# An expert layer with one first-stage product: relu(x(w1-w2)) w_out + x(w2 w_out) in place of max(x w1, x w2) w_out

## The chip, the core and the metric

One core of a Trainium2 chip runs the whole kernel. The metric is the device time of one execution in microseconds (us). TensorE (PE) multiplies, VectorE (DVE) and ScalarE (ACT) move results out of PSUM and do elementwise work, GpSimd (POOL) and SyncE (SP) here mostly issue DMAs; ACT issues DMAs as well. Each engine takes its instructions in the order of the program.

## The reference

Two layers run one after the other. First an attention in blocks: 4 batches of 8 heads, 768 positions of 64 numbers, in 8 blocks of 96. A small 8x8 matrix P for each head, normalised five times by rows and columns (Sinkhorn), mixes the blocks of K and V, and each block of Q attends to its mixed block.

```python
k_sorted = np.einsum('bhij,bhjcd->bhicd', P, k_b)    # and v_sorted
scores = scale * np.matmul(q_b, k_sb.transpose(0, 1, 2, 4, 3))
attn = softmax(scores)                               # by rows
x = np.matmul(attn, v_sb)  ->  (4*768 tokens, 8*64)
```

Then an expert layer on the 3072 tokens of 512 numbers, with w1 and w2 of 512x1024 and w_out of 1024x512:

```python
h1 = x @ w1
h2 = x @ w2
g = np.maximum(h1, h2)
return (g @ w_out).astype(np.float32)
```

Since max(a, b) = relu(a - b) + b, the result is also relu(x(w1 - w2)) w_out + x(w2 w_out).

## The kernel before

All matmuls take bf16 and add up in float32. There are 32 heads, four batches of eight; a "head" below is one of them, numbered from 0 in each batch.

**Sort.** For 16 heads at a time (batches 0 and 1, then 2 and 3) K and V lie as 128 rows of 6144 numbers. `emit_sort_batch` loads them in three pieces of 2048 (`k_ld`, `v_ld`, three buffers each, on POOL's queue), multiplies each piece by the block diagonal matrix `bd` of all P in four matmuls of 512 columns (`sort_ps`, line 164), casts the result (`k_ck` on ACT, line 176; `v_ck` on DVE, line 179; four buffers each) and stores it to DRAM (`k_sorted_dram` by SP's queue, `v_sorted_dram` by ACT's). "The second V sort" is the V part of the second group of 16 heads.

**Attention.** `emit_attention_group` loads the Q, K and V blocks of a head (`q_grp` on POOL, `k_grp` on SP, `v_grp` on ACT, six buffers each), transposes Q and K on TensorE in four small matmuls each (`tq_ps`, `tk_ps`) and copies them out on DVE (`qT`, `kT`). Then for the even and for the odd blocks it makes scores (`sc_ps`, four matmuls), the exp on ACT (`e_sb`), the output with a column of row sums (`o_ps`, four matmuls) and normalises on DVE into `x_stage`. That is 24 small matmuls a head. After the eight heads of a batch `emit_x_transpose` puts x into `xT` (32 transposes).

**Expert layer.** It goes by six chunks of 512 tokens. A chunk has eight first-stage units (`emit_moe_h`): four matmuls of 512 columns for `h1_ps` (line 305), four for `h2_ps` (line 313), a cast of the first on ACT (line 321) and the maximum on DVE (line 323). Then it has four output units (`emit_moe_out`) of eight matmuls each (line 331), a copy on ACT and a store. While heads run, up to two units are put into each head, one after the even blocks and one at the end, as soon as the tokens of their chunk are complete:

```python
moe_units.append(("h", tci, fi, (tci + 1) * TCH))
...
for h in range(H):
    emit_attention_group(b * H + h, x_stage, lambda: emit_avail_moe(avail_tokens, 1))
    emit_avail_moe(avail_tokens, 1)
emit_x_transpose(b, x_stage)
```

By that rule batch 0 has none, batches 1, 2 and 3 have 12, 16 and 16 units (32 of the first stage and 12 outputs in all), and the last 28 (four outputs of chunk 3, chunks 4 and 5) come after all heads: the tail.

**What sets the order.** The code is written in the order above (six Q loads, both sorts, two Q loads, the weight loads, then the batches), and the framework's scheduler puts the instructions of each engine into an order of its own, which is fixed before the run; waits are by semaphores. The weights are loaded on POOL's queue between the K and V loads: `w_sb0` to `w_sb3` hold 128 rows each of w1 (line 115) and w2 (line 118), `wout0` to `wout7` those of w_out (line 123). A DMA that is issued also waits until an earlier one in its lane of eight has landed.

Of the kernel before, what the change touches and what calls it, by code (L numbers as in the profile page):

```python
# [10 lines left out]
FP32 = mybir.dt.float32  # L11
BF16 = mybir.dt.bfloat16
# [3 lines left out]
def kernel(  # L16
# [11 lines left out]
    nc = tc.nc  # L28
    AF = mybir.ActivationFunctionType
    ALU = mybir.AluOpType  # L30
# [10 lines left out]
    DMODEL = H * D  # L41
    DFF = moe_w1.shape[1]
# [7 lines left out]
    TCH = 512  # L50
    NTCH = NTOK // TCH
    NFT = DFF // 128
# [7 lines left out]
    ident = const.tile([128, 128], BF16, tag="ident")  # L60
# [8 lines left out]
    for it in range(5):  # L69
# [4 lines left out]
            out=p_sb, in0=p_sb, in1=rowsum.to_broadcast([G, NB, NB]), op=ALU.mult  # L74
# [4 lines left out]
            out=p_sb,  # L79
            in0=p_sb,  # L80
            in1=colsum.to_broadcast([G, NB, NB]).transpose([0, 2, 1]),
            op=ALU.mult,
# [9 lines left out]
    for g in range(G):  # L92
        t, gl = divmod(g, GB)
        eng = nc.sync if g % 2 == 0 else nc.scalar
        eng.dma_start(
            out=bd_tiles[t][8 * gl : 8 * gl + 8, 8 * gl : 8 * gl + 8],
            in_=p2_bf[g : g + 1, :, :],
# [3 lines left out]
    xT = xt_pool.tile([128, 4, NTOK], BF16, tag="xT")  # L101

    wpool = ctx.enter_context(tc.tile_pool(name="wpool", bufs=1))
    w_sb = []
# [3 lines left out]
    wout_sb = []  # L108
# [4 lines left out]
    def emit_weight_loads():  # L113
        for dmt in range(4):
            nc.gpsimd.dma_start(
                out=w_sb[dmt][:, 0:DFF], in_=moe_w1[dmt * 128 : (dmt + 1) * 128, :]
            )
            nc.gpsimd.dma_start(
                out=w_sb[dmt][:, DFF : 2 * DFF],
                in_=moe_w2[dmt * 128 : (dmt + 1) * 128, :],  # L120
            )
        for ft in range(8):
            nc.gpsimd.dma_start(
                out=wout_sb[ft], in_=moe_w_out[ft * 128 : (ft + 1) * 128, :]
            )
# [5 lines left out]
    with tc.tile_pool(name="a_chunk", bufs=4) as chunk_pool, \  # L131
# [165 lines left out]

        moe_g_tiles = {}

        def emit_moe_h(tci, fi):  # L300
            tok0 = tci * TCH
            h1_ps = big_psum.tile([128, TCH], FP32, tag="big", name="h1_ps")
            h2_ps = big_psum.tile([128, TCH], FP32, tag="big", name="h2_ps")
            for dmt in range(4):
                nc.tensor.matmul(  # L305
                    h1_ps,
                    w_sb[dmt][:, fi * 128 : (fi + 1) * 128],
                    xT[:, dmt, tok0 : tok0 + TCH],
                    start=(dmt == 0),
                    stop=(dmt == 3),  # L310
                )
            for dmt in range(4):
                nc.tensor.matmul(  # L313
                    h2_ps,
                    w_sb[dmt][:, DFF + fi * 128 : DFF + (fi + 1) * 128],
                    xT[:, dmt, tok0 : tok0 + TCH],
                    start=(dmt == 0),
                    stop=(dmt == 3),
                )
            h1_sb = g_pool.tile([128, TCH], BF16, tag="h1_sb", name="h1_sb", bufs=3)  # L320
            nc.scalar.copy(out=h1_sb, in_=h1_ps)  # L321
            g_sb = g_pool.tile([128, TCH], BF16, tag="g_sb", name="g_sb")
            nc.vector.tensor_tensor(out=g_sb, in0=h2_ps, in1=h1_sb, op=ALU.max)  # L323
            moe_g_tiles.setdefault(tci, []).append(g_sb)

        def emit_moe_out(tci, tsi):
            tok0 = tci * TCH
            g_tiles = moe_g_tiles[tci]
            o_ps = obout_psum.tile([128, DMODEL], FP32, tag="obout", name="moe_o_ps")
            for fi in range(NFT):  # L330
                nc.tensor.matmul(  # L331
                    o_ps,
                    g_tiles[fi][:, tsi * 128 : (tsi + 1) * 128],
                    wout_sb[fi],
                    start=(fi == 0),
                    stop=(fi == NFT - 1),
                )
            o_sb = moe_out_pool.tile([128, DMODEL], FP32, tag="o_sb", name="o_sb")
            nc.scalar.copy(out=o_sb, in_=o_ps)  # L339
            row0 = tok0 + tsi * 128  # L340
            out_eng = nc.sync if tsi % 2 == 0 else nc.scalar
            out_eng.dma_start(out=out[row0 : row0 + 128, :], in_=o_sb)
# [8 lines left out]
        def emit_moe_unit(u):  # L351
            kind, tci, idx, _ = u
            if kind == "h":
                emit_moe_h(tci, idx)
            else:
                emit_moe_out(tci, idx)
# [18 lines left out]
        for g_pre in range(6, 8):  # L375
            emit_q_load(g_pre)
        emit_weight_loads()
        for b in range(B):
            x_stage = xstage_pool.tile(
                [BLK, NB, DMODEL], BF16, tag="x_stage", name="x_stage"  # L380
            )
            avail_tokens = b * S
            for h in range(H):
                emit_attention_group(
                    b * H + h, x_stage,
                    lambda: emit_avail_moe(avail_tokens, 1),
                )
                emit_avail_moe(avail_tokens, 1)
            emit_x_transpose(b, x_stage)
# [31 lines left out]
```

## Time and profile before

| what | value |
|---|---|
| median of three runs | 294.71 us (292.66 to 296.38) |
| span of the profiled execution, first to last instruction | 290.0 us |
| TensorE busy | 211.6 us, 73% of the span |
| VectorE busy | 116.6 us, 40% |
| ScalarE busy | 99.3 us, 34% |
| mean granted TensorE clock | 0.870 of full speed |

The time of a run includes a few us around the span: the median of the three runs is 4.7 us above the span of the profiled one, whose own time as a run is not listed. Busy shares are means over stages that have different limits, so they are read by stage. "Granted clock" is TensorE's: 1.00 is 2.4 GHz, 0.50 is 1.2 GHz.

### The profile page before, as it was taken

The numbers are of one execution on the slowest core, as the hardware profiler recorded it, in microseconds if no ns is written. First come the engines' busy times: TensorE is split into PE (matmuls) and PEld (weight loads), VectorE is DVE, ScalarE is ACT, GpSimd is POOL, SyncE is SP. The second block draws the span as 40 slices with busy tenths as digits, with TensorE's granted clock in tenths as the row PEclk, the third lists the DMA queues.
The fourth block names the chain that finished last, engine by engine and source line by source line (L and its number), as shares of the span: only waits on it lengthen the run. The fifth ranks groups of instructions, "written<-read, shape, count | busy, mean of one in ns | idle before, by whom it ended". The sixth has DMA issues, their size and how long they took to land.

```text
span 290.0 us, 4264 instructions
## 1 busy us (share of the span) xinstructions
PE 211.6 (73%) x1520; PEld 107.2 (37%) x1520; DVE 116.6 (40%) x393; ACT 99.3 (34%) x198; POOL 40.4 (14%) x66
## 2 busy tenths in 40 slices
PE   0001424235238589998879999999999999999994
PEld 0000000012024365554446455455455554444441
DVE  5400004323027872675352756365645640430320
ACT  2000421003312235434346343357444374333322
POOL 8300402106320121112111212112000000000000
PEclk9999955557555755999997999999999999999999
DMA  9993699999999997546883465754421003003003
GB/s 66 176 213 63 124 218 260 218 180 187 220 219 232 187 139 61 58 57 68 128 141 43 54 70 54 147 109 48 51 75 72 2 0 132 14 0 146 0 27 120
DMA packets 90245, 31.75 MB, mean 109 GB/s; under 512 B 77424, under 2 KB 84592, under 8 KB 90224
## 3 DMA queue, kind: packets, MB, share of 16 engines
q0 software_dynamic: 29120, 12.59, 36.2%
q1 hardware_dynamic: 30576, 9.45, 14.7%
q10 hardware_dynamic: 30528, 9.44, 14.4%
q8 instruction: 12, 0.20, 0.3%
q14 instruction: 9, 0.07, 0.1%
HBM read 31.47 MB, written 12.58 MB: 152 GB/s over the span
## 4 chain that ended last, share of the span: by engine, by line
PE 61%; DMA 24%; DVE 6%; ACT 5%; issue 2%; ACTq 1%; SPq 0%; DVEq 0%
PE h_ps L305 15%; PE moe_o_ps L331 15%; PE h_ps L313 14%; DMA k_sorted_dram<-k_ck 8%; PE o_ps L264 5%; DMA bd<-p_bf 5%; PE sc_ps L252 5%; DMA v_grp<-v_sorted_dram 4%; DMA k_grp<-k_sorted_dram 4%; PE xt_ps L287 3%; DMA v_sorted_dram<-v_ck 2%; PE tk_ps L236 2%; ACT e_sb L260 2%; DVE v_ck L179 1%; ACT k_ck L176 1%
## 5 line engine op out<-in xcount | busy, mean ns | idle before, releaser
L305 PE MATMUL h_ps<-xT,w_sb 128*128 128x512 bf16 x192 | 55.2, 390 | 0.0
L323 DVE TENSOR_TENSOR g_sb<-h_ps,h_sb 128x512 bf16<-128x512 f32 x48 | 33.1, 691 | 53.6 <-PE h_ps L313 51.6
L313 PE MATMUL h_ps<-xT,w_sb 128*128 128x512 bf16 x192 | 53.0, 380 | 0.0
L260 ACT ACTIVATE e_sb<-sc_ps 96x384 bf16<-96x384 f32 x64 | 30.1, 486 | 47.0 <-PE sc_ps L252 34.2
L331 PE MATMUL moe_o_ps<-wout,g_sb 128*128 128x512 bf16 x192 | 44.5, 379 | 0.7 <-ACT o_sb L339 0.7
L321 ACT CAST h_sb<-h_ps 128x512 bf16<-128x512 f32 x48 | 28.2, 588 | 47.8 <-PE h_ps L305 47.6
L164 PE MATMUL sort_ps<-k_ld,bd 128*128 128x512 bf16 x24 | 12.1, 562 | 37.3 <-DMA bd<-p_bf 20.3
L264 PE MATMUL o_ps<-v_grp,e_sb 96*96 96x65 bf16 x256 | 24.7, 224 | 11.6 <-DMA v_grp<-v_sorted_dram 6.4
L203 POOL DMA_DIRECT2D q_grp<-in_q_dram x24 | 18.5, 773 | 104.0 <-PE tq_ps L224 60.4
L179 DVE CAST v_ck<-sort_ps 128x512 bf16<-128x512 f32 x24 | 15.6, 685 | 41.7 <-PE sort_ps L164 34.7
L264 PEld LDWEIGHTS <-e_sb 96*96 96x96 bf16 x256 | 19.9, 138 | 30.1 <-ACT e_sb L260 13.9
L176 ACT CAST k_ck<-sort_ps 128x512 bf16<-128x512 f32 x24 | 13.3, 589 | 44.8 <-DMA bd<-p_bf 19.6
L274 DVE TENSOR_TENSOR x_stage<-o_ps,rs_sb 96x256 bf16<-96x256 f32 x64 | 26.7, 418 | 1.1
L331 PEld LDWEIGHTS <-g_sb 128*128 128x128 bf16 x192 | 18.4, 98 | 21.3 <-issue 1.6
L339 ACT COPY o_sb<-moe_o_ps 128x512 f32<-128x512 f32 x24 | 14.1, 586 | 35.2 <-PE moe_o_ps L331 35.1
L164 PEld LDWEIGHTS <-bd 128*128 128x128 bf16 x48 | 5.4, 121 | 51.8 <-issue 51.6
L313 PEld LDWEIGHTS <-w_sb 128*128 128x128 bf16 x192 | 17.5, 98 | 16.7 <-issue 0.2
L272 DVE COPY rs_sb<-o_ps 96x4 f32<-96x4 f32 x64 | 9.7, 153 | 32.3 <-PE o_ps L264 31.9
L305 PEld LDWEIGHTS <-w_sb 128*128 128x128 bf16 x192 | 17.2, 101 | 13.2 <-issue 0.3
L252 PE MATMUL sc_ps<-qT,kT 64*96 64x96 bf16 x256 | 19.0, 228 | 2.0 <-DVE kT L245 2.0
L252 PEld LDWEIGHTS <-kT 64*96 64x96 bf16 x256 | 12.8, 132 | 17.4 <-DVE kT L245 11.1
L233 DVE COPY qT<-tq_ps 128x384 bf16<-128x384 bf16 x32 | 11.1, 348 | 19.4 <-PE tq_ps L224 19.4
(33 smaller groups left out, 144.5 us busy)
## 6 DMA issues: line engine op xcount, KB each, us to landing
q_grp<-in_q_dram POOLq DMA_DIRECT2D x32, 96.0 KB, 3.3
k_ld<-in_k_dram POOLq DMA_DIRECT2D x6, 512.0 KB, 8.6
v_ld<-in_v_dram POOLq DMA_DIRECT2D x6, 512.0 KB, 11.0
k_sorted_dram<-k_ck SPq DMA_DIRECT2D x24, 128.0 KB
v_sorted_dram<-v_ck ACTq DMA_DIRECT2D x24, 128.0 KB
k_grp<-k_sorted_dram SPq DMA_DIRECT2D x32, 96.0 KB
v_grp<-v_sorted_dram ACTq DMA_DIRECT2D x32, 96.0 KB
out_dram<-o_sb SPq DMA_DIRECT2D x12, 256.0 KB
```

The source lines that it names most:

```text
L164: nc.tensor.matmul(ps, bd_tiles[t], ld[:, sub * SORT_CHUNK : (sub + 1) * SORT_CHUNK], start=True, stop=True,)
L179: nc.vector.tensor_copy(out=ck, in_=ps)
L203: nc.gpsimd.dma_start(out=q_grp, in_=q_g[g].rearrange("(j c) d -> c j d", j=NB))
L252: nc.tensor.matmul(sc_ps[:, sub, :], kT[ii * D : (ii + 1) * D, pr, :], qT[ii * D : (ii + 1) * D, pr, :], start=(sub == 0), stop=(sub == 3),)
L260: nc.scalar.activation(out=e_sb, in_=sc_ps, func=AF.Exp, scale=scale)
L264: nc.tensor.matmul(o_ps[:, sub, :], e_sb[:, sub, :], v_grp[:, i, :], start=(sub == 0), stop=(sub == 3),)
L274: nc.vector.tensor_tensor(out=x_stage[:, par:NB:2, h * D : (h + 1) * D], in0=o_ps[:, :, 0:D], in1=rs_sb.to_broadcast([BLK, 4, D]), op=ALU. ...
L305: nc.tensor.matmul(h1_ps, w_sb[dmt][:, fi * 128 : (fi + 1) * 128], xT[:, dmt, tok0 : tok0 + TCH], start=(dmt == 0), stop=(dmt == 3),)
L313: nc.tensor.matmul(h2_ps, w_sb[dmt][:, DFF + fi * 128 : DFF + (fi + 1) * 128], xT[:, dmt, tok0 : tok0 + TCH], start=(dmt == 0), stop=(dmt ...
L321: nc.scalar.copy(out=h1_sb, in_=h1_ps)
L323: nc.vector.tensor_tensor(out=g_sb, in0=h2_ps, in1=h1_sb, op=ALU.max)
L331: nc.tensor.matmul(o_ps, g_tiles[fi][:, tsi * 128 : (tsi + 1) * 128], wout_sb[fi], start=(fi == 0), stop=(fi == NFT - 1),)
```

## The change

The kernel computes w1 - w2 (in place of w1) and w2 w_out once on the chip. `emit_weight_algebra` stands after the weight loads and ahead of the first batch: for each of eight column blocks of w2 four transposes on TensorE (`tw_ps`, line 308) and a copy to `w2T` on DVE (line 316); then for each 128 rows of w2 eight matmuls of 512 columns that give w2 w_out (`c_ps`, line 322), a cast to `wc` on ACT (line 330), and a subtraction on DVE (line 332). A first-stage unit then has four matmuls and one elementwise step, relu on ACT (line 352) for even units and the maximum with zero on DVE for odd ones. An output unit has twelve matmuls: four of `xT` with `wc` (line 364), and the eight with w_out as before (line 372).

```diff
+        w2T = wpool.tile([128, NFT, DMODEL], BF16, tag="w2T", name="w2T")
+        wc_sb = []
+
+        def emit_weight_algebra():
+            for fi in range(NFT):
+                tw_ps = trsc_psum.tile([128, 4, 128], BF16, tag="trsc", name="tw_ps")
+                for dmt in range(4):
+                    nc.tensor.matmul(
+                        tw_ps[:, dmt, :],
+                        w_sb[dmt][:, DFF + fi * 128 : DFF + (fi + 1) * 128],
+                        ident,
+                        is_transpose=True,
+                        start=(dmt == 0),
+                        stop=(dmt == 3),
+                    )
+                nc.vector.tensor_copy(
+                    out=w2T[:, fi, :].rearrange("p (t d) -> p t d", d=128), in_=tw_ps
+                )
+            for dmt in range(4):
+                c_ps = big_psum.tile([128, DMODEL], FP32, tag="big", name="c_ps")
+                for fi in range(NFT):
+                    nc.tensor.matmul(
+                        c_ps,
+                        w2T[:, fi, dmt * 128 : (dmt + 1) * 128],
+                        wout_sb[fi],
+                        start=(fi == 0),
+                        stop=(fi == NFT - 1),
+                    )
+                wc = wpool.tile([128, DMODEL], BF16, tag=f"wc{dmt}", name=f"wc{dmt}")
+                nc.scalar.copy(out=wc, in_=c_ps)
+                wc_sb.append(wc)
+                nc.vector.tensor_tensor(
+                    out=w_sb[dmt][:, 0:DFF],
+                    in0=w_sb[dmt][:, 0:DFF],
+                    in1=w_sb[dmt][:, DFF : 2 * DFF],
+                    op=ALU.subtract,
+                )
+
         def emit_moe_h(tci, fi):
             tok0 = tci * TCH
-            h1_ps = big_psum.tile([128, TCH], FP32, tag="big", name="h1_ps")
-            h2_ps = big_psum.tile([128, TCH], FP32, tag="big", name="h2_ps")
+            h_ps = big_psum.tile([128, TCH], FP32, tag="big", name="h_ps")
...
-            for dmt in range(4):
-                nc.tensor.matmul(
-                    h2_ps,
-                    w_sb[dmt][:, DFF + fi * 128 : DFF + (fi + 1) * 128],
-                    xT[:, dmt, tok0 : tok0 + TCH],
-                    start=(dmt == 0),
-                    stop=(dmt == 3),
-                )
-            h1_sb = g_pool.tile([128, TCH], BF16, tag="h1_sb", name="h1_sb", bufs=3)
-            nc.scalar.copy(out=h1_sb, in_=h1_ps)
             g_sb = g_pool.tile([128, TCH], BF16, tag="g_sb", name="g_sb")
-            nc.vector.tensor_tensor(out=g_sb, in0=h2_ps, in1=h1_sb, op=ALU.max)
+            if fi % 2 == 0:
+                nc.scalar.activation(out=g_sb, in_=h_ps, func=AF.Relu)
+            else:
+                nc.vector.tensor_scalar(
+                    out=g_sb, in0=h_ps, scalar1=0.0, scalar2=None, op0=ALU.max
+                )
...
             o_ps = obout_psum.tile([128, DMODEL], FP32, tag="obout", name="moe_o_ps")
+            for dmt in range(4):
+                nc.tensor.matmul(
+                    o_ps,
+                    xT[:, dmt, tok0 + tsi * 128 : tok0 + (tsi + 1) * 128],
+                    wc_sb[dmt],
+                    start=(dmt == 0),
+                    stop=False,
+                )
             for fi in range(NFT):
...
         emit_weight_loads()
+        emit_weight_algebra()
         for b in range(B):
```

The scheduler makes a new order of it. Three places carry the steps of the prediction.

On TensorE in the opening, before: the last matmuls of the first V sort, with head 0's K transposes and scores (`k_grp_493`, `kT_510`) among them.

```order
L164 MATMUL sort_ps_325<-v_ld_318,bd0_107 128x512
L236 LDWEIGHTS k_grp_493
L236 MATMUL tk_ps_505<-ident_58,k_grp_493 128x96
...
L164 MATMUL sort_ps_330<-v_ld_318,bd0_107 128x512
L252 LDWEIGHTS kT_510
L252 MATMUL sc_ps_512<-qT_503,kT_510 96x96
...
L164 MATMUL sort_ps_335<-v_ld_318,bd0_107 128x512
```

And after, on TensorE, from the same sort to head 0's first transpose (`w_sb1` and `w_sb3` are the second and the last quarter of w1 and w2, `q_grp_197` is head 0's Q):

```order
L164 MATMUL sort_ps_331<-v_ld_319,bd0_107 128x512
L308 LDWEIGHTS w_sb1_151
L308 MATMUL tw_ps_493<-ident_58,w_sb1_151 128x128
...
L164 MATMUL sort_ps_336<-v_ld_319,bd0_107 128x512
...
L308 LDWEIGHTS w_sb3_153
L308 MATMUL tw_ps_493<-ident_58,w_sb3_153 128x128
...
L164 MATMUL sort_ps_402<-k_ld_385,bd1_109 128x512
L224 LDWEIGHTS q_grp_197
L224 MATMUL tq_ps_595<-ident_58,q_grp_197 128x96
```

Head 0 has moved from among the first V sort to behind the whole second K sort and all transposes of w2, and the first V sort's last matmul now stands behind transposes that need the second quarter of w2.

On TensorE at the end of the second V sort, before (`e_sb_670` is head 3, `kT_714` head 4 of batch 0):

```order
L164 MATMUL sort_ps_467<-v_ld_450,bd1_109 128x512
L264 LDWEIGHTS e_sb_670
L264 MATMUL o_ps_672<-v_grp_648,e_sb_670 96x65
...
L252 LDWEIGHTS kT_714
L252 MATMUL sc_ps_716<-qT_707,kT_714 96x96
```

And after (`e_sb_681` is head 1, `kT_709` head 2; between the first and the last row of `c_ps` lie 30 more pairs of that kind):

```order
L164 MATMUL sort_ps_468<-v_ld_451,bd1_109 128x512
L264 LDWEIGHTS e_sb_681
L264 MATMUL o_ps_683<-v_grp_643,e_sb_681 96x65
...
L322 LDWEIGHTS w2T_196
L322 MATMUL c_ps_541<-wout0_154,w2T_196 128x512
...
L322 MATMUL c_ps_577<-wout7_161,w2T_196 128x512
L252 LDWEIGHTS kT_709
L252 MATMUL sc_ps_711<-qT_702,kT_709 96x96
```

All 32 matmuls of w2 w_out stand in one block, and two more heads of batch 0 stand behind the second V sort than before.

On ScalarE (which issues V requests) around the end of the second K sort, before (`v_grp_597` is head 2's V):

```order
L176 CAST k_ck_393<-sort_ps_391 128x512
L176 CAST k_ck_398<-sort_ps_396 128x512
L176 CAST k_ck_403<-sort_ps_401 128x512
L215 DMA v_grp_597<-v_sorted_dram_165 96x8x64
L181 DMA v_sorted_dram_165<-v_ck_410 128x512
```

And after (`v_grp_694` is head 2's V, `v_grp_745` head 3's):

```order
L176 CAST k_ck_389<-sort_ps_387 128x512
L215 DMA v_grp_694<-v_sorted_dram_165 96x8x64
L215 DMA v_grp_745<-v_sorted_dram_165 96x8x64
L176 CAST k_ck_394<-sort_ps_392 128x512
L176 CAST k_ck_399<-sort_ps_397 128x512
L176 CAST k_ck_404<-sort_ps_402 128x512
L260 ACTIVATE e_sb_614<-sc_ps_609 96x384
```

The requests for the V blocks of heads 2 and 3 have moved ahead of the last three K casts.

## Rows read from the trace of the kernel before

**Rows 1.** The page, parts 1 and 2: span, busy time, granted clock in 40 slices
```profile
span 290.0 us, 4264 instructions
...
PE 211.6 (73%) x1520; PEld 107.2 (37%) x1520; DVE 116.6 (40%) x393; ACT 99.3 (34%) x198; POOL 40.4 (14%) x66
...
PEclk9999955557555755999997999999999999999999
```

**Rows 2.** Busy times by stage, us in all and busy in the stretch
```profile
core 0: us, PE busy (x) PEld busy (x) DVE busy (x) ACT busy (x) POOL busy (x), PEclk, DMA share, GB/s
99.50:109.50 10.00, 8.76 (x101) 7.26 (x101) 7.15 (x38) 3.46 (x8) 2.31 (x3) 0.50 1.79 133
113.30:133.00 19.70, 19.70 (x148) 9.82 (x146) 11.64 (x38) 7.99 (x16) 3.09 (x4) 0.95 0.59 62
...
206.00:238.00 32.00, 31.79 (x273) 16.56 (x272) 17.95 (x59) 14.30 (x30) 0.00 (x0) 1.00 0.12 37
238.50:286.00 47.50, 47.50 (x221) 21.32 (x218) 11.06 (x16) 16.61 (x30) 0.00 (x0) 1.00 0.15 58
```

**Rows 3.** Chain that ended last, in the tail: start us, us, what
```profile
279.11 6.92 PE moe_o_ps L331 x32
```

**Rows 4.** The same chain in batch 1, one step of each head
```profile
119.24 0.17 PE tq_ps L224 x4
...
124.39 0.17 PE tq_ps L224 x4
...
129.42 0.17 PE tq_ps L224 x4
```

**Rows 5.** Groups by line: busy us, mean ns of one | idle before
```profile
L323 DVE TENSOR_TENSOR g_sb<-h_ps,h_sb 128x512 bf16<-128x512 f32 x48 | 33.1, 691 | 53.6 <-PE h_ps L313 51.6 <-ACT e_sb L260 1.3
...
L321 ACT CAST h_sb<-h_ps 128x512 bf16<-128x512 f32 x48 | 28.2, 588 | 47.8 <-PE h_ps L305 47.6 <-DVE rs_sb L273 0.2
...
L179 DVE CAST v_ck<-sort_ps 128x512 bf16<-128x512 f32 x24 | 15.6, 685 | 41.7 <-PE sort_ps L164 34.7 <-DMA v_sorted_dram<-v_ck 6.0 <-DMA v_grp<-v_sorted_dram 0.5
...
L164 PE MATMUL sort_ps<-v_ld,bd 128*128 128x512 bf16 x24 | 12.7, 594 | 7.7 <-DVE v_ck L179 4.2 <-ACT k_ck L176 3.4
```

**Rows 6.** The chain in the opening
```profile
63.06 0.51 PE tk_ps L236 x4
...
78.23 9.80 DMA v_grp<-v_sorted_dram
...
110.94 2.01 PE xt_ps L287 x20
...
113.34 0.43 PE h_ps L305
```

**Rows 7.** Timeline of TensorE in the opening: start us, us [idle before]
```profile
25.15 1.44 PE L164 MATMUL sort_ps<-k_ld,bd 128*128 128x512 bf16 x3 [20.29 <-DMA bd<-p_bf]
...
95.98 0.38 PE L164 MATMUL sort_ps<-v_ld,bd 128*128 128x512 bf16 x1 [0.17 <-DVE v_ck L179]
...
104.71 0.57 PE L252 MATMUL sc_ps<-qT,kT 64*96 64x96 bf16 x8 [0.15 <-DVE kT L245]
...
107.20 0.57 PE L252 MATMUL sc_ps<-qT,kT 64*96 64x96 bf16 x8 [0.15 <-DVE kT L245]
```

**Rows 8.** Timeline of POOL, and the landing of w2's quarters (line 118)
```profile
48.26 0.55 POOL L118 DMA_DIRECT2D w_sb<-in_moe_w_dram  x1
...
65.74 0.54 POOL L159 DMA_DIRECT2D v_ld<-in_v_dram  x1 [12.57 <-PE sort_ps L164]
...
68.10 0.57 POOL L118 DMA_DIRECT2D w_sb<-in_moe_w_dram  x1
...
DMA to landing us min/median/max: 9.4/10.3/11.9
```

**Rows 9.** Timeline of VectorE, second V sort, first and last cast of 12
```profile
87.17 0.69 DVE L179 CAST v_ck<-sort_ps 128x512 bf16<-128x512 f32 x1 [0.49 <-DMA v_grp<-v_sorted_dram]
...
97.77 0.69 DVE L179 CAST v_ck<-sort_ps 128x512 bf16<-128x512 f32 x1 [0.64 <-DMA v_sorted_dram<-v_ck]
```

More of the change, by code (lines that the diff above doesn't have):

```diff
@@ L298 @@
         moe_g_tiles = {}
+        w2T = wpool.tile([128, NFT, DMODEL], BF16, tag="w2T", name="w2T")
[34 more added lines that the diff above has]
+                )
         def emit_moe_h(tci, fi):
             tok0 = tci * TCH
-            h1_ps = big_psum.tile([128, TCH], FP32, tag="big", name="h1_ps")
-            h2_ps = big_psum.tile([128, TCH], FP32, tag="big", name="h2_ps")
+            h_ps = big_psum.tile([128, TCH], FP32, tag="big", name="h_ps")
             for dmt in range(4):
                 nc.tensor.matmul(
-                    h1_ps,
+                    h_ps,
                     w_sb[dmt][:, fi * 128 : (fi + 1) * 128],
@@ L311, in emit_moe_h @@
                 )
-            for dmt in range(4):
-                nc.tensor.matmul(
-                    h2_ps,
-                    w_sb[dmt][:, DFF + fi * 128 : DFF + (fi + 1) * 128],
-                    xT[:, dmt, tok0 : tok0 + TCH],
-                    start=(dmt == 0),
-                    stop=(dmt == 3),
-                )
-            h1_sb = g_pool.tile([128, TCH], BF16, tag="h1_sb", name="h1_sb", bufs=3)
-            nc.scalar.copy(out=h1_sb, in_=h1_ps)
-            g_sb = g_pool.tile([128, TCH], BF16, tag="g_sb", name="g_sb")
-            nc.vector.tensor_tensor(out=g_sb, in0=h2_ps, in1=h1_sb, op=ALU.max)
+            g_sb = g_pool.tile([128, TCH], BF16, tag="g_sb", name="g_sb")
+            if fi % 2 == 0:
[3 more added lines that the diff above has]
+                    out=g_sb, in0=h_ps, scalar1=0.0, scalar2=None, op0=ALU.max
+                )
             moe_g_tiles.setdefault(tci, []).append(g_sb)
@@ L334, in emit_moe_out @@
                     wout_sb[fi],
-                    start=(fi == 0),
+                    start=False,
                     stop=(fi == NFT - 1),
```

## The prediction

> **What bounds the kernel now.** I read the page's busy times and the row of the granted clock first, then the busy times by stage, then the chain that ended last, and then the waits of the opening stage.
>
> The page alone says little: TensorE is busy 73% of 290.0 us [rows 1]. By stage it says where the rest lies. From 113 us on TensorE hardly waits: it is busy for 19.70 of 19.70 us at the start of batch 1, for 31.79 of 32.00 late in the heads, and for 47.50 of 47.50 in the tail, where only expert work is left [rows 2]. There is no stage like that before 113 us: the chain goes from one DMA to the next (head 0's K blocks let TensorE go on at 63.06, V blocks asked for at 78.23 take 9.80 us) [rows 6]. So two different kernels stand one after the other: an opening of 113 us that waits for transfers, mostly at half clock, and 177 us that wait for TensorE. The change takes TensorE work out of the second and puts TensorE work into the first.
>
> **Expert layer, matmuls.** In the tail 32 matmuls of 512 columns take 6.92 us, 0.216 us each [rows 3]; that is the price of one wherever the clock is full. Before, a chunk of 512 tokens has 8 units of 8 matmuls and 4 output units of 8: 96. Afterwards it has 8 of 4 and 4 of 12: 80. Six chunks: 576 becomes 480, 96 fewer, **-20.7 us** if TensorE bounds all of them. Of this the tail holds two whole chunks and the four output units of chunk 3: 224 matmuls become 208, -3.5 us, and since TensorE never waits there, I take it as certain. The other 80 (-17.3 us) lie in batches 1 to 3, as two unequal parts: 32 units of the first matmul stage lose 4 matmuls each (-27.6), 12 output units gain 4 each (+10.4).
>
> **What fills the gap in a head.** Batches 1 to 3 offer two places for expert units in each head. A head with two units of the first stage takes 5.15 and 5.03 us (119.24 to 124.39 to 129.42 [rows 4]), 5.09 in the mean: 16 large matmuls are 3.46 us, the 24 small ones of attention 1.63. Afterwards 8 large ones are 1.73, and the head 3.36 us, if nothing else is late. What could be late is the head's own chain (copy of the transposed K, scores, exp, output, normalising). With no expert work beside it such a head takes 2.49 us at half the clock (scores at 104.71 and 107.20 [rows 7]). A head cannot be slower than that chain and its 8 matmuls in a row: 2.49 + 1.73 = 4.22 us, 0.86 above 3.36. For 16 such heads the price of new gaps is between 0 and 13.8 us. I take 0.2 us a head, **+3.2 us**: in the new order the 8 large matmuls stand between the transposes of K and the scores, so they cover the copy, which is the longest link; and VectorE has 7.15 us for four heads [rows 2], 1.79 a head, to which one cast of 0.69 comes, 2.5 of 3.36 us.
>
> A rule of the Trainium skill speaks against this small price. The page "Trainium Kernel Development and Optimization", section "Performance Expectations", says that matmul busy time is a bad measure of how near a kernel is to its roofline, because matmuls are pipelined. The rows agree in part: in the tail busy time is real work (512 columns in 0.216 us), but 24 matmuls of 96 columns would need 24 x 0.216 x 96/512 = 0.97 us by that rate, and take 1.63. By the rule, then, 0.66 us of each head is waiting that looks busy, and as much again could come to light when half the cover goes: 16 x 0.66 = 10.6 us in place of my 3.2, and 293.3 us in place of 285.9.
>
> **The casts.** Before, each unit has a cast on ScalarE (588 ns) and a maximum on VectorE (691 ns) [rows 5]. Afterwards it has one or the other: relu on ScalarE, priced as that cast, or a maximum with zero on VectorE, priced as the V cast of the same shape (685 ns). Both run beside TensorE, which has 1.73 us for two units; I count nothing. If that cover failed, the 24 units of one engine could cost 24 x 0.69 at most, and no row hints at it. In the tail, too, a unit has 0.86 us of matmuls beside one cast. One PSUM buffer a unit in place of two only loosens things.
>
> **The opening.** Added to it: 32 transposes of w2, 8 copies of them on VectorE, 32 matmuls of 512 columns for w2 w_out, 4 casts on ScalarE, and 4 subtractions on VectorE. Twenty transposes of x took 2.01 us [rows 6], so 32 are 3.2 to 4.3 us (128 columns in place of 96). A copy lies between half and the whole of the 0.69 us V cast: 3 to 5.5 us, beside the transposes. No row has a subtraction from SBUF to SBUF of 128x1024; between one and two of the 0.69 us operations, four cost 2.8 to 5.5 us, in time in which VectorE waits for landings anyway.
>
> The place matters more than the price, since engines take their work in order. (1) The first three groups of transposes stand among the sort matmuls and wait for w2. Its last quarter is asked for at 68.10 us, behind a V load that waited 12.57 us for the sort matmul after head 0's K transposes [rows 8]. In the new order those are gone from there, and that load waits for the second quarter of w2 instead: asked for near 48 [rows 8], landed 10.3 us later, near 58.5. So the last quarter is asked for near 62.5 and lands near 73 [rows 8]. (2) Behind it come 5 us of transposes and copies, and only then head 0, near 78 to 80, with the last K sort matmuls between. Before, head 0's K was transposed at 63.06 [rows 6]; little is lost by that, since the chain then stood until V blocks landed at 88.03 [rows 6]. (3) The 12 casts of the second V sort took from 87.17 to 98.46 us [rows 9], and the last sort matmul stood at 95.98 [rows 7]. Afterwards it is at the earliest 78 + 10 = 88, and at the latest 99, where the V blocks land no sooner than now, at 88, and the 11.3 us follow. On ScalarE's queue the request for head 3's V blocks now stands ahead of three K casts, and waits for an earlier landing of about 10 us; so I take the later half, **94**. (4) Here the new order puts all 32 matmuls of w2 w_out, ahead of head 2's scores. At the full clock they take 6.9 us. Three sort matmuls at half clock took 1.44 us [rows 7], 0.59 of it the last one [rows 5], so 0.43 from one to the next: 13.7 us. The clock is half in most of the opening (PEclk [rows 1]), and it came up for good when the first dense expert matmuls ran; I take **10**. (5) Before, four heads were left at 95.98; now six are left behind the 32 matmuls. From the scores of the last head to the first expert matmul went 113.34 - 107.20 = 6.14 us; with five periods of 2.49 that is 18.6. At full clock a head can come down to VectorE's 1.79: 14. I take **18**.
>
> The expert layer then starts at 94 + 10 + 18 = 122 us in place of 113.34: **+8.7 us**. Its bounds are 88 + 6.9 + 14 = 109 (-4.4) and 99 + 13.7 + 18.6 = 131.3 (+18).
>
> **Sum.** -20.7 + 3.2 + 8.7 = -8.8 us: a span of 281.2. The profiled span is 290.0; the median of the three runs, 294.71, is 4.7 above it, which I keep: **285.9, say 286 us**, 3% faster. Two per cent, 5.9 us, is about what a measurement of this kernel can tell from no change.
>
> **Rivals.** *The opening gives it all back.* The 32 matmuls run at half clock throughout (13.7) and the V sort ends where it does now (97), then 18.6: the expert layer starts at 129.3, +16, and -20.7 + 3.2 + 16 = -1.5: 293 us, no change. For it: the clock is at half from 36 to 116 us but for two slices [rows 1], and every step of the opening waits for a landing. Against it: TensorE then has 32 large matmuls in a row with all operands on hand.
>
> *The clock falls in the thinner heads* (slower). Large matmuls are 68% of a head now (3.46 of 5.09) and would be 51%. Between 99.5 and 109.5 us, with attention alone, TensorE was 88% busy and granted 0.50 throughout [rows 2]; so being busy is not enough. At half clock a head would take 2.49 + 8 x 0.43 = 5.9 us in place of 3.36, 2.55 more. From 4 such heads on the gain is gone; from 6 the kernel is slower by over 2%; with half of the 16, 286 + 20 = 306 us. Against it: the start of batch 1 was granted 0.95 in the mean and late heads 1.00, and from 116 us on there is one dip alone [rows 1, 2].
>
> *The algebra hides in waits.* TensorE has idle time in the opening; if the V sort ends at 90, the run takes 7 and the heads 16.3, the start stays at 113.3, and -17.5 gives 277 us. That the change misses what it says is out: in the new order each unit has 4 matmuls and each output 12.
>
> **Chances.** Forecast (281 to 293 us) 0.59; all given back (290 to 295) 0.20; hidden (275 to 280) 0.12; clock (above 296) 0.09. About three quarters of the forecast's range lies below 288.8, where 2% begins: faster 0.45 + 0.12 + 0.02 = 0.59, same 0.14 + 0.18 = 0.32, slower 0.09. The range must take in the given-back case and half of the hidden one: 277 to 297.
>
> **What would show it.** The tail's expert matmuls should be 208, and the heads with two first-stage units should take 3.3 to 3.8 us; 4.2 would be the price by the chain. The first expert matmul should stand at 122 us (113 hidden, 129 given back), the 32 matmuls should take 7 to 14 us, and PEclk in batches 1 to 3 should be near 1.00. I am wrong in mechanism if the opening moves by less than 3 us, if the clock falls among the heads, or if a transfer of K or V blocks bounds the faster heads.

## The result, and the profile after

| kernel | time, us (median, lowest to highest) | span of the profiled execution | first expert matmul at | from there to the end |
|---|---|---|---|---|
| before | 293.69 (291.39 to 296.38, 4 runs) | 290.0 | 113.14 | 176.9 |
| after | 281.9 (281.45 to 282.27, 4 runs) | 278.5 | 122.06 | 156.4 |

The ratio is 0.9619 (95% interval 0.9573 to 0.9666): 3.8% faster, where 286 us was forecast. The first expert matmul is dated by the timeline of TensorE here; the chain of [rows 6] puts that of before 0.2 us later. Executions that took over 1.5% longer than the fastest of the same kernel (one of the kernel before here; one of no_tr, two of relu_act and three of sort2_relu_act below) are left out of the ratios and not of the medians.

The page of the changed kernel, parts 1 and 2, against [rows 1]:

```profile
span 278.5 us, 4087 instructions
...
PE 195.5 (70%) x1466; PEld 101.6 (36%) x1488; DVE 104.3 (37%) x381; ACT 86.4 (31%) x178; POOL 40.4 (15%) x66
...
PEclk9999999999999597559999799999999989999999
```

By its records TensorE is busy for 16 us less, and its share of the span has fallen. By the page alone one would not say that the kernel is still bound by it. The busy times cut at the first expert matmul say more. First the kernel before, opening and rest:

```profile
0.00:113.14 113.14, 43.50 (x277) 21.80 (x277) 36.63 (x135) 25.57 (x54) 26.56 (x48) 0.69 1.07 175
113.14:290.00 176.86, 168.11 (x1247) 85.36 (x1244) 79.94 (x258) 73.73 (x146) 13.88 (x18) 0.98 0.39 67
```

And the changed kernel (columns as in [rows 2]; from 231 us on it is the tail):

```profile
0.00:122.06 122.06, 51.99 (x344) 25.75 (x347) 43.17 (x148) 27.86 (x58) 26.75 (x49) 0.91 0.91 163
122.06:278.50 156.44, 143.47 (x1126) 75.87 (x1143) 61.15 (x233) 58.58 (x120) 13.65 (x18) 0.97 0.45 76
...
231.00:278.50 47.50, 43.31 (x198) 19.54 (x200) 5.53 (x8) 12.25 (x21) 0.00 (x0) 1.00 0.18 67
```

The rest is 20.4 us shorter and the opening 8.9 us longer, against -17.5 and +8.7 in the forecast. (This trace lacks 22 matmul records, as 1466 matmuls beside 1488 weight loads on its page show; 21 of them are large ones of the rest, whose busy time is some 4.5 us low for that.) The opening, on the timeline of TensorE:

```profile
74.99 0.58 PE L164 MATMUL sort_ps<-k_ld,bd 128*128 128x512 bf16 x1 [11.94 <-ACT k_ck L176]
...
92.48 0.58 PE L164 MATMUL sort_ps<-v_ld,bd 128*128 128x512 bf16 x1 [0.51 <-DVE v_ck L179]
93.61 8.92 PE L322 MATMUL c_ps<-wout,w2T 128*128 128x512 bf16 x31
102.46 0.39 PE L252 MATMUL sc_ps<-qT,kT 64*96 64x96 bf16 x8
...
122.06 1.48 PE L343 MATMUL h_ps<-xT,w_sb 128*128 128x512 bf16 x3
```

Against [rows 7]: the second V sort ends at 93.1 us, the block of w2 w_out takes 8.9 (31 of its 32 matmuls are recorded), and six heads and the transposes of x take 19.6. The forecast had 94, 10 and 18. Heads and tail, on the chain that ended last, against [rows 3] and [rows 4]:

```profile
159.31 0.32 PE sc_ps L252 x8
162.58 0.32 PE sc_ps L252 x8
164.77 0.38 PE sc_ps L252 x8
168.75 0.38 PE sc_ps L252 x8
171.55 0.38 PE sc_ps L252 x8
...
239.99 6.91 PE h_ps L343 x32
```

Four heads of batch 2 take 12.24 us, 3.06 each, where the heads of [rows 4] took 5.09. The scheduler no longer gives each head the same share (10, 5, 12 and 6 large matmuls between these scores, 33 in all), so only the mean counts. In the tail a large matmul still takes 0.216 us.

### The profile page after: what moved, and what is told of

It reads as the page before. It is cut to its first block, busy times and chain, and to the rows that moved or that the text cites. A ratio compares the mean times of both kernels' runs of the same rounds, so it can differ in the third digit from the quotient of the medians.

```text
span 278.5 us, 4087 instructions
## 1 busy us (share of the span) xinstructions
PE 195.5 (70%) x1466; PEld 101.6 (36%) x1488; DVE 104.3 (37%) x381; ACT 86.4 (31%) x178; POOL 40.4 (15%) x66
## 4 chain that ended last, share of the span: by engine, by line
PE 56%; DMA 22%; DVE 9%; ACT 8%; issue 2%; ACTq 1%; SPq 0%; DVEq 0%
PE moe_o_ps L372 15%; PE h_ps L343 14%; DMA k_grp<-k_sorted_dram 8%; PE moe_o_ps L364 8%; DMA bd<-p_bf 5%; PE o_ps L264 5%; DMA k_sorted_dram<-k_ck 4%; PE sc_ps L252 4%; DMA v_sorted_dram<-v_ck 4%; PE c_ps L322 3%; ACT e_sb L260 3%; PE xt_ps L287 2%; ACT k_ck L176 2%; PE tk_ps L236 2%; DVE v_ck L179 1%
## 5 line engine op out<-in xcount | busy, mean ns | idle before, releaser
L343 PE MATMUL h_ps<-xT,w_sb 128*128 128x512 bf16 x178 | 48.5, 391 | 0.4
L372 PE MATMUL moe_o_ps<-wout,g_sb 128*128 128x512 bf16 x188 | 45.9, 381 | 0.2
L260 ACT ACTIVATE e_sb<-sc_ps 96x384 bf16<-96x384 f32 x64 | 28.2, 483 | 28.3 <-PE sc_ps L252 22.8
L179 DVE CAST v_ck<-sort_ps 128x512 bf16<-128x512 f32 x24 | 15.9, 687 | 45.5 <-PE sort_ps L164 33.4
L354 DVE TENSOR_SCALAR g_sb<-h_ps 128x512 bf16<-128x512 f32 x24 | 16.5, 689 | 37.3 <-PE h_ps L343 36.0
L372 PEld LDWEIGHTS <-g_sb 128*128 128x128 bf16 x192 | 18.8, 98 | 22.2
L364 PE MATMUL moe_o_ps<-wc,xT 128*128 128x512 bf16 x93 | 24.9, 384 | 1.0 <-ACT o_sb L380 0.6
L343 PEld LDWEIGHTS <-w_sb 128*128 128x128 bf16 x192 | 17.6, 101 | 13.9 <-issue 0.8
L352 ACT ACTIVATE g_sb<-h_ps 128x512 bf16<-128x512 f32 x24 | 14.2, 598 | 23.6 <-PE h_ps L343 19.6
L164 PE MATMUL sort_ps<-v_ld,bd 128*128 128x512 bf16 x24 | 11.6, 513 | 13.1 <-DVE v_ck L179 9.8
L252 PE MATMUL sc_ps<-qT,kT 64*96 64x96 bf16 x256 | 13.4, 223 | 4.7 <-DVE kT L245 4.3
L296 ACT COPY xT<-xt_ps 128x384 bf16<-128x384 bf16 x32 | 13.3, 505 | 6.8 <-PE xt_ps L287 6.5
```

The costliest lines, as they stand in the source:

```text
L164: nc.tensor.matmul(ps, bd_tiles[t], ld[:, sub * SORT_CHUNK : (sub + 1) * SORT_CHUNK], start=True, stop=True,)
L179: nc.vector.tensor_copy(out=ck, in_=ps)
L252: nc.tensor.matmul(sc_ps[:, sub, :], kT[ii * D : (ii + 1) * D, pr, :], qT[ii * D : (ii + 1) * D, pr, :], start=(sub == 0), stop=(sub == 3),)
L260: nc.scalar.activation(out=e_sb, in_=sc_ps, func=AF.Exp, scale=scale)
L343: nc.tensor.matmul(h_ps, w_sb[dmt][:, fi * 128 : (fi + 1) * 128], xT[:, dmt, tok0 : tok0 + TCH], start=(dmt == 0), stop=(dmt == 3),)
L354: nc.vector.tensor_scalar(out=g_sb, in0=h_ps, scalar1=0.0, scalar2=None, op0=ALU.max)
```

## The experiments

Each was timed beside the kernel before, in three groups of four on a chip each: no_c, no_tr, layer_only and c_twice; out8, cast_dve, fill_c and sort2_late; the other four. The kernel before took 293.70, 292.98 and 292.74 us there, so medians of different groups compare to about 1 us. Ratios are to the kernel before in the same group; the changed kernel's own is 0.9619. The last two columns are of the profiled execution, in us.

| run | median, us | ratio, 95% interval | first expert matmul | from there to the end |
|---|---|---|---|---|
| no_c | 276.22 | 0.9421 (0.9358 to 0.9484) | 117.66 | 158.5 |
| no_tr | 283.78 | 0.9689 (0.9631 to 0.9747) | 122.17 | 156.2 |
| layer_only | 274.40 | 0.9358 (0.9312 to 0.9404) | 116.08 | 156.5 |
| c_twice | 288.93 | 0.9853 (0.9788 to 0.9919) | 129.09 | 156.3 |
| alg_only | 303.30 | 1.0361 (1.0329 to 1.0393) | 124.28 | 176.5 |
| out8 | 261.25 | 0.8931 (0.8893 to 0.8969) | 123.1 | 136.8 |
| cast_dve | 286.87 | 0.9823 (0.9775 to 0.9871) | 122.8 | 161.8 |
| relu_act | 282.61 | 0.9567 (0.9520 to 0.9615) | 124.87 | 154.3 |
| fill_c | 278.38 | 0.9531 (0.9480 to 0.9581) | 118.12 | 157.6 |
| sort2_late | 265.69 | 0.9100 (0.9050 to 0.9149) | 103.64 | 158.2 |
| before_sort2 | 284.53 | 0.9705 (0.9652 to 0.9757) | 109.61 | 174.1 |
| sort2_relu_act | 264.39 (260.43 to 265.86) | none | 103.19 | 155.2 |

**Layer without algebra, algebra without layer.**

```diff
# layer_only, against the changed kernel
-            for fi in range(NFT):
-                tw_ps = trsc_psum.tile([128, 4, 128], BF16, tag="trsc", name="tw_ps")
...
-                c_ps = big_psum.tile([128, DMODEL], FP32, tag="big", name="c_ps")
...
-                nc.scalar.copy(out=wc, in_=c_ps)
+                nc.scalar.copy(out=wc, in_=wout_sb[dmt])
-                nc.vector.tensor_tensor(
-                    out=w_sb[dmt][:, 0:DFF],
...
# alg_only, against the kernel before
         emit_weight_loads()
+        emit_weight_algebra()
```

> The whole algebra is left out (w1 stands in for w1-w2, the first four row blocks of w_out for w2 w_out), so the output is not the reference's; the expert layer has its 480 matmuls. Theory and rival A: the start is at 113 to 115 us and the run takes 273 to 275 us, 96 x 0.216 = 20.7 us below the kernel before if nothing new waits in the heads. Rival B (the thinner heads have new waits that the earlier start would bring out): 276 us or more with the start at 113.

> The kernel before, with the algebra added ahead of the first batch as in the changed kernel (its results, w1-w2 in a tile of its own, are not used). Theory (the algebra moves the opening by its 32 matmuls less what waits there in any case, 6 to 9 us, and nothing else): first expert matmul near 122, 300 to 303 us. Rival (the 20 us of the expert layer depend on the opening, since what the late start delays comes back as fuller heads): 294 to 298 us.

The busy times from the first expert matmul to the end, first of the layer without algebra:

```profile
116.08:272.60 156.52, 143.58 (x1126) 76.03 (x1143) 61.20 (x233) 58.54 (x120) 13.62 (x18) 0.97 0.46 76
```

Then of the algebra in the kernel before:

```profile
124.28:300.80 176.52, 165.31 (x1220) 84.81 (x1239) 79.58 (x257) 73.21 (x144) 13.61 (x18) 0.98 0.39 68
```

This is the cleanest reading of the study. With the old layer the rest is 176.9 and 176.5 us, with the new one 156.5 and 156.4, whether the algebra is there or not. The layer is worth 20.0 to 20.4 us of the rest, close to the 20.7 of 96 matmuls at 0.216, and the algebra acts on the opening alone. (By the medians the layer is worth 19.3 us without the algebra and 21.4 with it, since the opening has another order each time.) Both rivals fall: the layer alone runs 274.4 us though its start, 116.08, is later than expected, and the algebra alone is not softened by what follows, but costs 10.6 us, more than expected.

**Which part of the algebra costs.**

```diff
# no_c
-                c_ps = big_psum.tile([128, DMODEL], FP32, tag="big", name="c_ps")
-                for fi in range(NFT):
-                    nc.tensor.matmul(
-                        c_ps,
...
-                nc.scalar.copy(out=wc, in_=c_ps)
+                nc.scalar.copy(out=wc, in_=w2T[:, 2 * dmt, :])
# no_tr
-            for fi in range(NFT):
-                tw_ps = trsc_psum.tile([128, 4, 128], BF16, tag="trsc", name="tw_ps")
...
-                        w2T[:, fi, dmt * 128 : (dmt + 1) * 128],
+                        w_sb[fi % 4][:, DFF + dmt * 128 : DFF + (dmt + 1) * 128],
# c_twice
-                for fi in range(NFT):
+                for rnd in range(2):
+                    for fi in range(NFT):
```

> The 32 matmuls of w2 w_out are left out: wc is cast from a piece of w2T, so the output is not the reference's; transposes, copies, casts and subtractions stay. Theory (the opening is late because these 32 matmuls stand as one block on TensorE's path, 8.9 us, ahead of head 2's scores): the first expert matmul stands at 113 us in place of 122.06, and the run takes about 273 us. Rival A (the opening is late because the transposes of w2 wait for its last quarter and push head 0 and the heads after it behind the V sort): the order of the heads is as in the changed kernel, so the start stays within 2 us of 122 and the run takes 280 to 282.

> The 32 transposes of w2 and their 8 copies are left out: the 32 matmuls take columns of w2 as they lie in place of the transposed ones, so the output is not the reference's. Theory (the block of 32 matmuls is the price): the expert layer still starts near 122 us, 282 us. Rival A (the transposes and their wait for w2 are the price): the start goes back to 113 to 115 us, 273 to 275 us.

> The 32 matmuls of w2 w_out are done twice over, into the same sums, so w2 w_out comes out doubled. Theory: every one of the 32 added is on the path, 6.9 us at full clock: start at 129, 289 us. Rival C (the block lies beside waits for transfers that end later anyway, or lifts the clock for the heads behind it): under 4 us more, 285 or less.

The timeline of TensorE with the block done twice, in which 62 of the 64 matmuls are recorded:

```profile
93.72 3.57 PE L323 MATMUL c_ps<-wout,w2T 128*128 128x512 bf16 x8
...
97.46 12.03 PE L323 MATMUL c_ps<-wout,w2T 128*128 128x512 bf16 x54 [0.17 <-issue]
109.42 0.39 PE L252 MATMUL sc_ps<-qT,kT 64*96 64x96 bf16 x8
...
129.09 1.48 PE L344 MATMUL h_ps<-xT,w_sb 128*128 128x512 bf16 x3
```

The 32 added matmuls cost 7.0 us in the start and 7.0 in the time: all of them are on the path, as the theory has it. Without the transposes nothing is won: the start is 122.17, and the time, 283.8, is no better than the 281.9 with them, so the forecast of rival A fails. But this does not show that the transposes are free, because no_tr has another order. From its timeline (the profiled execution, at 280.18 us, was the fastest of five):

```profile
63.73 0.50 PE L236 MATMUL tk_ps<-ident,k_grp 96*128 96x96 bf16 x4 [8.37 <-DMA k_grp<-k_sorted_dram]
...
100.66 0.38 PE L164 MATMUL sort_ps<-v_ld,bd 128*128 128x512 bf16 x1 [0.60 <-DVE v_ck L179]
101.26 7.07 PE L307 MATMUL c_ps<-wout,w_sb 128*128 128x512 bf16 x31 [0.22 <-DVE v_ck L179]
```

Head 0's K transposes are back at 63.73, the second V sort ends 8 us later than in the changed kernel, the block takes 7.07 us in place of 8.92, and four heads stand behind it, not six. That the start comes out the same is the sum of these. no_c against layer_only, timed beside each other, says more: with transposes, copies and subtractions but without the block the start is 1.6 us later and the time 1.8 us longer, and the intervals of the two overlap. So what the transposes cost by their place is small, and not shown to be more than nothing.

Without the block the start comes back by 4.4 us and the time by 5.7, not by the 8.9 that the block lasts; neither forecast for no_c holds. (Its profiled execution was the slowest of four, 278.0 us, and its rest is 2.1 us longer than the changed kernel's.) The timeline without the block:

```profile
93.30 0.63 PE L164 MATMUL sort_ps<-v_ld,bd 128*128 128x512 bf16 x1
97.11 0.57 PE L252 MATMUL sc_ps<-qT,kT 64*96 64x96 bf16 x8 [0.91 <-DVE kT L245]
...
117.66 1.05 PE L334 MATMUL h_ps<-xT,w_sb 128*128 128x512 bf16 x2
```

Head 2's scores then start 3.8 us after the last sort matmul starts, not right behind it, because its chain is not ready: the block covers that. From those scores to the first expert matmul it is 20.6 us without the block and 19.6 with it, where the first scores behind the block are short (0.39 us for eight in place of 0.57): the block left TensorE at full clock for about three heads. So 8.9 us of work cost some 5.

**What bounds the expert layer now.**

```diff
# out8
-            for dmt in range(4):
-                nc.tensor.matmul(
-                    o_ps,
-                    xT[:, dmt, tok0 + tsi * 128 : tok0 + (tsi + 1) * 128],
-                    wc_sb[dmt],
...
# cast_dve: every unit takes the branch of VectorE
-            if fi % 2 == 0:
+            if False:
# relu_act: every unit takes that of ScalarE
-            if fi % 2 == 0:
+            if True:
```

> The four matmuls of x with w2 w_out are left out of each of the 24 output units (the w2 part of the result is missing); order and opening are those of the changed kernel. Theory (from the first expert matmul to the end TensorE is the bound, at 0.216 us a large matmul, in the heads too): 96 matmuls fewer, -20.7 us, 261 us. Rival (in the heads another step, the head's chain or a cast, now ends last): only the 48 matmuls of the 12 outputs of the tail count, -10.4, 271 to 272 us.

> All 48 casts of the first stage are made on VectorE, 24 more of 0.69 us there and 24 fewer on ScalarE. Theory (casts lie beside TensorE): within 1 us of the changed kernel's 281.9. Rival (a head with two units takes 3.06 us now and VectorE would have 1.79 + 2 x 0.69 = 3.17 us in it, so the cast is the next bound): 0.1 to 0.7 us for each of 16 heads, 284 to 293 us.

> All 48 casts of the first stage are made by relu on ScalarE. Theory (the casts all on VectorE cost 5 us because VectorE's own work in a head, 1.79 us, leaves it no room; ScalarE has two exps of 0.49 us, 0.98, and has room): 279 to 282 us, no slower than the changed kernel. Rival (any single engine that takes all casts holds up a PSUM buffer, whatever its load): 285 us or more, as with VectorE.

The outputs without their 96 added matmuls run 20.65 us faster, 0.215 us each (19.6 us in the rest of the profiled executions): TensorE still sets the pace, in the heads as in the tail. The casts are not free wherever they stand. All on VectorE, 5.0 us are lost, and the rival's forecast holds. All on ScalarE, the interval overlaps the changed kernel's, and the rival there, 285 us or more, falls: that one engine has all the casts is not what costs. The rest of that profiled execution is 154.3 us in place of 156.4. That is not shown to be the casts either: batch 1 is 1.4 us longer there, and batch 3, which was granted 1.00 there and 0.95 in the changed kernel, 3.1 us shorter. The busy times of batches 1 and 2 and of the tail, with all casts on VectorE:

```profile
122.80:161.30 38.50, 34.26 (x305) 18.69 (x304) 19.69 (x80) 12.20 (x29) 6.16 (x8) 0.90 0.71 90
161.30:201.60 40.30, 38.35 (x337) 19.99 (x335) 24.52 (x88) 12.26 (x28) 6.16 (x8) 0.97 0.70 88
...
237.00:284.60 47.60, 43.60 (x202) 19.59 (x200) 11.07 (x16) 7.77 (x14) 0.00 (x0) 0.99 0.18 66
```

And the same two batches of the changed kernel:

```profile
122.06:157.00 34.94, 31.22 (x294) 18.06 (x297) 17.18 (x75) 14.23 (x31) 5.93 (x8) 0.94 0.77 99
157.00:194.20 37.20, 36.19 (x332) 19.87 (x337) 20.29 (x80) 16.61 (x37) 6.18 (x8) 0.98 0.71 93
```

The loss lies in the heads, 3.6 and 3.1 us in these two batches (batch 3 gains 1.4 back, 35.4 in place of 36.8); the tail, where VectorE has nothing but the casts, takes 47.6 us in place of 47.5. VectorE is busy for only 61% of batch 2 even so. A mean share does not tell when an engine's steps have to be done. The scheduler also laid the units out differently, so the 5 us are not shown to be VectorE's load alone.

**Other places for the work.**

```diff
# fill_c: the products as fillers of batch 0's heads
+        fill_slots = {6: [("c", 0)], 8: [("c", 1)], 10: [("c", 2)], 12: [("c", 3)]}
# sort2_late (on the changed kernel), before_sort2 (on the kernel before)
-        emit_sort_batch(1)
...
             emit_x_transpose(b, x_stage)
+            if b == 0:
+                emit_sort_batch(1)
# sort2_relu_act: sort2_late and all first-stage casts on ScalarE
```

> The four products of w2 w_out are written as fillers of batch 0's heads, so that 14 of the 32 matmuls stand ahead of head 2's scores and 18 between the steps of heads 2 to 4. Theory (the block costs because TensorE can do nothing else in it, while the heads of batch 0 have idle TensorE time in their chain): the expert layer starts at 118 to 119 us in place of 122, 278 to 279 us. Rival (TensorE is as good as full in those heads): no change, 281 to 283 us.

> The second sort (heads of batches 2 and 3) is written behind batch 0, so that its loads follow those of the weights and its matmuls stand among batch 0's heads; the algebra stands ahead of all heads. Theory (the opening is bound by transfers, and the second sort's are not needed before 157 us): the expert layer starts at 100 to 112 us, and the rest keeps 156 us and a few more for casts and stores that now lie in batch 1: 262 to 273 us. Rival (the transfers, busy to 103 us in any order, hold the heads up all the same): start at 118 or later, 279 us or more.

> The kernel before, with the second sort written behind batch 0, and no algebra. Theory (with the second sort late the algebra lies in waits, so there the change is worth its whole 96 x 0.216 = 20.7 us): 283 to 288 us, against the 265.7 of the changed kernel with the same move. Rival (the algebra costs the same 6 to 9 us there): 276 to 280 us.

> The second sort written behind batch 0 and all casts of the first stage on ScalarE. Theory (VectorE also has the casts of the second V sort, which now lie in batches 0 and 1): 262 to 266 us, a gain of up to 3 over the same kernel with casts shared. Rival (ScalarE, which issues the V stores and requests, is held up by the casts): 268 us or more.

As fillers, the products win 3.5 us: start at 118.12, as expected, with 18 of the 32 matmuls inside the chain of three heads. That is within 0.5 us of the start without any products (no_c). The two intervals just touch, but the slowest of its four executions, 280.35 us, is faster than the fastest of the changed kernel, 281.45. The larger prize is the order of the sorts. With the second sort behind batch 0, the timeline of TensorE reads:

```profile
67.64 5.99 PE L322 MATMUL c_ps<-wout,w2T 128*128 128x512 bf16 x27
73.47 0.34 PE L224 MATMUL tq_ps<-ident,q_grp 96*128 96x96 bf16 x4
...
103.64 1.27 PE L343 MATMUL h_ps<-xT,w_sb 128*128 128x512 bf16 x3
```

The block stands directly ahead of head 0, the second sort's matmuls fill the heads, and the expert layer starts 18 us earlier; from there to the end it is 158.2 us, 1.8 more than without that move. At 265.7 us this beats both kernels, by 9.0% and 5.8%. How much of it is transfers is not shown, because the move took matmuls, casts and stores along with the loads. The kernel before with the same move has 284.5: so the move is worth 8.2 us there and 16.2 on the changed kernel, and the change is worth 18.8 us with it and 11.8 without. The time of before_sort2 lies in its theory's range, but that the algebra then costs nothing is not shown. The first expert matmul is 6.0 us earlier with the change and the rest 15.9 us shorter, because the two orders differ: before_sort2 puts batch 1's first heads and the end of the second sort ahead of its first expert matmul. Its transposes of batch 0's x end at 99.6 us, those of sort2_late at 102.8, so some 3 us of the algebra may be paid there too. With all casts on ScalarE as well, the rest of the profiled run is 155.2 us, 3.0 less; but the runs spread from 260.4 to 265.9 us, there is no ratio, and the gain in time stays open.

## Why the prediction was right, step by step

**Two kernels, one behind the other.** Right. The split at the first expert matmul, opening bound by transfers and rest by TensorE, is what alg_only and layer_only separate to within 0.4 us. That transfers bound the opening is read from its waits and holds up to the second V sort alone: behind it 32 more matmuls were paid in full (c_twice).

**The expert matmuls, -20.7 us.** Right: -20.4 between the two profiles, and layer_only and out8 give the same price a matmul. From the last transposes of x on, the tail lasts 47.7 us (230.76 to 278.5) in place of 51.6 (238.37 to 290.0), 3.9 less. Six of its 208 matmuls stand ahead of that point, and four of its 224 before, so 18 fewer are left: 3.9 us at 0.216.

**The gaps, +3.2 us.** This is the term that was mis-sized: net it is +0.3 (20.7 less 20.4). New waits did come, at the size that I gave. TensorE's waits from the first expert matmul to the last head, in the kernel before (113.4 to 239 us):

```profile
PE sc_ps L252 <- DVE kT L245: 1.5, 2, 1.0
PE o_ps L264 <- ACT e_sb L260: 1.3, 3, 0.5
PE xt_ps L287 <- DVE x_stage L274: 0.9, 2, 0.6
PE moe_o_ps L331 <- ACT o_sb L339: 0.7, 2, 0.3
```

And in the changed kernel (122 to 232 us; five more of 0.2 to 0.5 us are left out):

```profile
PE o_ps L264 <- ACT e_sb L260: 2.7, 8, 0.5
PE sc_ps L252 <- DVE kT L245: 1.3, 1, 1.3
PE xt_ps L287 <- DVE x_stage L274: 1.2, 3, 0.5
PE moe_o_ps L364 <- ACT o_sb L380: 0.6, 2, 0.3
```

That is 4.4 us before and 7.2 after, +2.8. What I had not seen is the other side. From the first expert matmul to the last transposes of x:

```profile
113.14:238.37 125.23, 120.46 (x1028) 63.95 (x1026) 68.88 (x242) 56.40 (x117) 13.88 (x18) 0.98 0.49 70
...
122.06:230.76 108.70, 99.92 (x928) 56.21 (x942) 55.61 (x225) 46.10 (x99) 13.65 (x18) 0.96 0.58 80
```

By their weight loads, 356 large matmuls lie in the first stretch and 278 in the second. At 0.216 us each they leave 48.33 and 48.65 us for everything else: +0.3, although the listed waits are 2.8 longer. So what looked like work of the small matmuls, with pauses too short to be listed, gave back some 2.5 us, 0.1 us a head.

The four heads above seem to say more: 33 large matmuls are 7.13 us of their 12.24, which leaves 1.28 a head, against 1.63 by [rows 4]. Such a head comes to 3.06 us, below the band of 3.3 to 3.8 that I gave, and far below the price by the chain, 4.22. But the kernel before has heads like that as well. Between these scores of its batch 3 lie 13 large matmuls each time, which leaves 1.34 and 1.33:

```profile
199.56 0.32 PE sc_ps L252 x8
...
203.71 0.32 PE sc_ps L252 x8
...
207.85 0.38 PE sc_ps L252 x8
```

So 1.63 us was not a constant of a head, and why it varies is open. The sum also took 8 large matmuls for each head with two units; the scheduler put none to 28 between the scores of one head and the next. The rule that I had weighed, of the Trainium skill's page "Trainium Kernel Development and Optimization", section "Performance Expectations", that matmul busy time is a bad measure, agrees with the 2.5 us. But my use of it had the wrong sign: the hidden waiting shrank, and 293.3 us by it was 11 too many. (Its 0.97 us also takes all 24 matmuls at 96 columns; eight, those of `o_ps`, have 65, which makes it 0.87.)

**The opening, +8.7 us.** Right in sum, 8.9, and in its three steps (93.1, 8.9, 19.6 against 94, 10, 18); that the sum fits to 0.2 us is luck, since the steps miss by -0.9, -1.1 and +1.6. Two things in it were wrong. Head 0 came at 81.68 us, not at 78 to 80, and not by the wait for w2, which was asked for at 59.41, even earlier than the 62.5 worked out from [rows 8], but by one that I had not foreseen (below). It cost nothing visible, because the V sort ends at much the same time in all: its last matmul stands at 92.5 to 96.1 us in the runs with the changed order (no_tr and the runs with the second sort late have another), and at 95.98 before. And the block's 8.9 us are not its price: with and without it the kernel differs by some 5, and the algebra as a whole costs 7.5 us in the new layer and 10.6 in the old one. The opening without any algebra does not go back to 113 but to 116.08, because five heads instead of four stand behind the second V sort there. Between 6 and 11 us I can't say how much is order and how much the sort's end, which moves by up to 3.6 us between the profiled executions of these kernels.

**The casts at nothing.** Close for the split that the change has; each lasts as priced, 598 ns on ScalarE and 689 on VectorE. But the cover on VectorE may be thinner than 2.5 of 3.36 us suggested: cast_dve lost 5.0 us, though its order differs too.

**From span to time.** I kept 4.7 us from the profiled span to the time. The run that was profiled took 281.45 us, 2.95 above its span, and the other three 1.8 to 2.5 above theirs. For the profiled run the forecast was 4.45 us too high: 2.7 of it is the span, that is the gaps, and 1.75 this term. The 4.7 set the median of three executions against the span of one, so it held their spread as well: in the 21 executions of the kernel before beside the experiments the time is 1.8 to 2.1 us above that execution's own span.

**The rivals.** The opening did not give all back (122.06, not 129.3), the algebra did not hide (not 113.3), and the clock did not fall in the heads at large: 0.97 from the first expert matmul on, against 0.98 before. It did fall once, ahead of the tail, after 4 us in which TensorE was busy for 1.86:

```profile
223.00:227.00 4.00, 1.86 (x33) 1.35 (x31) 2.78 (x13) 0.86 (x2) 0.00 (x0) 1.00 0.01 4
227.00:231.00 4.00, 3.78 (x30) 2.40 (x29) 0.31 (x1) 3.10 (x8) 0.00 (x0) 0.57 0.00 0
```

Batch 3 of the kernel before was granted 1.00. An estimate of what the dip cost is 1.7 us at most (0.43 of 4.00), and it lies inside the 48.65 us above.

## What to carry to other kernels

Cut the profile where the bound changes, and price each part of a change by the stage that it lands in: 96 matmuls were worth 20.0 to 20.4 of their 20.7 us where TensorE is the bound. Of 32 matmuls put as one block into a stage that waits for transfers some 5 of 8.9 us were paid, and 32 more behind them were paid in full, so what a block costs depends on what it covers; as fillers among the heads they cost 3.5 us less. When a stage waits for transfers, ask which of them are needed there at all: moving the second sort was worth 16.2 us on the changed kernel, more than the change, and 8.2 on the kernel before, less than it. So the two are worth more together than apart, some 27 us in place of 20; the reason was not looked into.

## What the runs showed that I had not expected

**A load's landing held up casts on ScalarE.** The timeline of ScalarE and its queue in the changed kernel:

```profile
51.05 23.19 ACTq L181 DMA_DIRECT2D v_sorted_dram<-v_ck  x6
74.35 0.59 ACT L176 CAST k_ck<-sort_ps 128x512 bf16<-128x512 f32 x1 [29.17 <-DMA k_grp<-k_sorted_dram]
```

ScalarE's queue holds V stores ahead of the K casts. The last of these six waited for the semaphore of its lane until 73.83 us, when the K block that SP had asked for at 51.89 in the same lane had landed. So the K cast behind it waited 29.17 us, and TensorE's sort matmul at 74.99 waited 11.94 us for that cast. Undoing that wait alone was not tried.

**TensorE's mean clock hardly shows in the time.** The four runs of the changed kernel had a mean granted clock of 0.944, 0.890, 0.944 and 0.890, and took 281.45, 282.27, 281.79 and 282.01 us. The opening of the profiled one was granted 0.91, that of the kernel before 0.69. In which stage the other three runs had less is not on record; single steps do depend on the clock, as the block of 32 matmuls, 8.92 us here and 7.07 in no_tr.
